# The attention's row stores of a fused attention and mixture-of-experts kernel, issued by ScalarE's queue in place of SyncE's

## The chip, the cores and the metric

The kernel runs on one core of a Trainium2 chip. The metric is the device time of one execution in microseconds (us): before the change it is 562.4 us, the median of 3 runs (560.54 to 562.91).

## The reference

An attention over 32 memory slots per head is computed first, then a top-1 mixture of experts on its output. Shapes: batch 8, 8 heads, 576 tokens, head size 64, so 4608 tokens of 512 numbers; 8 experts with a hidden size of 1024.

```python
a = softmax(phi, axis=2)                       # [8, 8, 576, 32]
k_m = einsum('bhsm,bhsd->bhmd', a, k)          # 32 keys and
v_m = einsum('bhsm,bhsd->bhmd', a, v)          # 32 values per head
attn = softmax(q @ k_m.T / 8)
x = (attn @ v_m).transpose(0, 2, 1, 3).reshape(4608, 512)

logits = x @ w_gate
e_idx = argmax(logits)
gate_w = softmax(logits)[e_idx]
eom = sigmoid(x @ w_output_gate)
for e in range(8):                             # each token goes to one expert
    mask = e_idx == e
    out[mask] = gate_w * eom[:, e] * (relu(x[mask] @ w1[e]) @ w2[e])
```

## The kernel before, in words

**Two parts.** The attention makes the rows of x. They go out to a scratch tensor `xs` in HBM, 576 numbers each (512 of x and gate columns), because the experts need the rows in another order: GpSimd gathers them again by indirect DMAs, sorted by expert (`gather`, L524). The experts' matmuls (`several`, L1216 on) take most of the span and run on TensorE nearly without a gap. The first of them are recorded while the attention's last quarter is still to be done, and the rest of the attention is woven into them by `hook`.

**The attention's loop.** The batch goes in four pairs (`bp`). For a pair, `memory(bp)` (L719) makes the memories: ScalarE takes exponentials of phi (`ph`, L711), TensorE transposes them (L735), ScalarE copies them out (`at`, L745, and `a`, L741 and L742), TensorE sums over the tokens (`sums`, L764, with the loaded keys and values `kvt`), ScalarE scales the sums (`kvm`, L781), TensorE turns them (L790), and ScalarE copies the keys out (`kT`, L795). Beside that runs the loop over 20 query tiles in `attention()` (L1113), five for a pair. One turn of it takes several tiles at different steps, in the order of the table `ORDER` (L35): exponentials (X, `ea`, L875), row maxima (S, L865 to L871), normalising (D, L881 to L884), transposing back (B, L889), the values of a tile in two halves (V0 and V1), and the scores of the next tile (C, L855, which waits for the loaded queries `qt`). M and m are steps of the memories, R steps of the routing, which VectorE and GpSimd do for the most part.

**The rows.** `values` (L892) multiplies a half tile on TensorE (L902) into a PSUM tile `bpd`, and ScalarE copies it to half of the tile `xo` in SBUF (L904). After V1, `store` (L1008) sends the whole `xo` to `xs`: one DMA of 128 partitions x 2 x 576 numbers, 576 KB (L1013), for four of a pair's five tiles, and two DMAs of 64 x 576, 144 KB each (L1017), for the fifth. There are 16 of the former and 8 of the latter. `xo` has two buffers, so the copies of a tile wait until the store of the tile two before has landed.

**What sets the order.** Each engine executes its own instructions in the order in which the code records them, and a waiting instruction holds back all behind it. Every load and store, other than GpSimd's indirect ones, is issued by SyncE (SP), and they run through one hardware queue: queries (`load_q`, L672), keys and values (`load_kv`, L677; a pair of 512 KB loads is issued after each `sums`, two pairs ahead of the one that is summed next), phi (L662), gate columns (L982 and L985, 64-byte pieces), and the experts' weights (L565). The stores stand among them where the code records them. Each such DMA takes the next of eight completion semaphores (DMAHW0 to DMAHW7 in the order's rows), and before it is issued it waits until the last DMA on that semaphore has landed; so at most eight are under way.

Of the kernel before, what the change touches and what calls it, by code (L numbers as in the profile page):

```python
# [17 lines left out]
P = 128  # L18
# [49 lines left out]
def attention_moe(tc, phiT, kv, qT, wgo, wall, out):  # L68
    nc = tc.nc
    V, A, G, T = nc.vector, nc.scalar, nc.gpsimd, nc.tensor  # L70

    with contextlib.ExitStack() as ctx:
        cp = ctx.enter_context(tc.tile_pool(name="cp", bufs=1))
        dp = ctx.enter_context(tc.tile_pool(name="dp", bufs=1, space=bass.MemoryType.DRAM))
        xs = dp.tile([NTOK, XROW], F32, name="xs")
# [932 lines left out]
        def store(bp, c2, xo, lg):  # L1008
            t0 = bp * 2 * S
            b, n = c2 // 2, 2 if c2 < 4 else 1  # L1010
            if c2 < 4:
                r = t0 + b * S + (c2 % 2) * 256
                nc.sync.dma_start(xs[r:r + 256].rearrange("(c p) d -> p c d", p=P),  # L1013
                                  xo[:].rearrange("p c r d -> p c (r d)"))
            else:
                for b_ in range(2):
                    nc.sync.dma_start(  # L1017
                        xs[t0 + b_ * S + 512:t0 + b_ * S + 576],
                        xo[64 * b_:64 * b_ + 64, 0].rearrange("p r d -> p (r d)"))
            xl = xo[:].rearrange("p c r (g d) -> p c (r g) d", g=2)[:, 0:n, :, P:XQ]  # L1020
            defer("lg", lambda: V.tensor_reduce(
                lg[:, 2 * c2:2 * c2 + n], xl.rearrange("p c q l -> p c l q"), axis=AX.X, op=ALU.add))
# [73 lines left out]
        def defer(nm, f):  # L1096
            deferred.append([LATE[nm], f])
# [15 lines left out]
        def attention():  # L1113
# [8 lines left out]
            for t in range(NT + LAG["V"]):  # L1122
                for w in ORDER:
# [8 lines left out]
                    elif w == "W":  # L1132

                        while t == START - 1 and stream.split(2):
                            pass
                    elif w == "V0" and 0 <= g < NT:
                        bp, c = g // 5, g % 5
                        while 2 * bp + (c >= 2) not in ves:
                            mem.step()
                        if g == 5 * bp:  # L1140
                            lgs[bp] = rt.tile([P, NCH, 16], F32, name="lg", bufs=2)
                        xo = wk.tile([P, 2, 2, 2 * XQ], F32, name="xo", bufs=2)
                        values(bp, 2 * c, st[g], xo)
                    elif w == "V1" and 0 <= g < NT:
                        if c < 4:
                            values(bp, 2 * c + 1, st[g], xo)
                        store(bp, c, xo, lgs[bp])
                    elif w == "C" and 0 < g < NT:
                        while 2 * (g // 5) + (g % 5 >= 2) not in kTs:
                            mem.step()  # L1150
                        st[g] = scores(g // 5, g % 5)
                        if g + NQ < NT:
                            load_q(g + NQ)
                    elif w == "S" and 0 <= g < NT:
                        shift(st[g])
                    elif w == "X" and 0 <= g < NT:
                        expo(st[g])
                    elif w == "D" and 0 <= g < NT:
                        divide(st[g])
                    elif w == "B" and 0 <= g < NT:  # L1160
                        back(st[g])
# [282 lines left out]
```

## Time and profile before

| what | value |
|---|---|
| runs | 560.54, 562.91, 562.4 us (median 562.4) |
| the profiled execution's own time | 555.65 us |
| its span on the core | 553.9 us |
| mean granted TensorE clock | 0.969 |
| busy in the span: TensorE, VectorE, ScalarE, GpSimd | 92%, 64%, 52%, 42% |
| moved by DMA | 123.54 MB, 223 GB/s on average |
| on the hardware queue, on GpSimd's queue | 102.71 MB, 20.06 MB |

The span is the profiled execution's on the core; its own time has 1.75 us around that. All rows below are of that one execution, which is 6.75 us shorter than the median of the runs. PE is TensorE's matmuls, PEld its weight loads, DVE VectorE, ACT ScalarE, POOL GpSimd, and SPq the sequencer of SyncE, which issues DMAs and does nothing else. L13 is line 13 of the kernel. A name such as `xo<-bpd` says that the instruction writes tile xo and reads tile bpd.

### The profile page before, as it was taken

How to read it: one execution, taken by the hardware profiler on the slowest of the kernel's cores; microseconds unless marked ns; L12 is line 12 of the kernel's file. 1: busy time of each engine (PE TensorE's matmuls, PEld its weight loads, DVE VectorE, ACT ScalarE, POOL GpSimd, SP SyncE). 2: the span in 40 equal slices, each digit the busy share in tenths (PEclk: the TensorE clock that was granted, in tenths of full speed). 3: DMA queues.
4: the chain of work that ended last, by engine and by line, in shares of the span. 5: the costliest groups of instructions: out<-in, count | busy, mean ns of one | idle time of the engine just before them, and what ended most of it. 6: DMA issues, size and time to landing. Idle time of an engine off the chain costs nothing. (4 is left out here: it accounts for less than half of the span.)

```text
span 553.9 us, 10578 instructions
## 1 busy us (share of the span) xinstructions
PE 509.0 (92%) x3859; PEld 437.6 (79%) x3859; DVE 352.0 (64%) x779; ACT 287.9 (52%) x536; POOL 232.6 (42%) x254
## 2 busy tenths in 40 slices
PE   3788877599999999999999999999999999999993
PEld 2455555388689799898998989897999899888982
DVE  4384979957776659996436556944786387549310
ACT  3475765454454446553435546834775377358310
POOL 2242585851434034410466562563447463710101
PEclk9877989979999999999999999999999999999997
DMA  8999999995457756963547574875586577643001
GB/s 310 416 389 392 411 373 400 320 351 175 132 192 240 225 168 222 309 183 115 154 139 259 174 233 126 262 219 182 179 264 177 190 244 241 201 162 98 30 21 43
DMA packets 41998, 123.54 MB, mean 223 GB/s; under 512 B 10256, under 2 KB 10320, under 8 KB 41552
## 3 DMA queue, kind: packets, MB, share of 16 engines
q1 hardware_dynamic: 35136, 102.71, 56.0%
q0 software_dynamic: 6800, 20.06, 10.3%
q8 instruction: 32, 0.52, 0.4%
q14 instruction: 30, 0.25, 0.1%
HBM read 102.40 MB, written 20.35 MB: 222 GB/s over the span
## 5 line engine op out<-in xcount | busy, mean ns | idle before, releaser
L1275 PE MATMUL bps<-whl,hh 128*128 128x512 f32 x640 | 193.6, 394 | 0.9 <-issue 0.9
L1238 PE MATMUL bps<-xh,whl 128*128 128x384 f32 x640 | 166.0, 336 | 0.0
L590 DVE TENSOR_TENSOR whl<-w,whl 128x1024 fp32r<-128x1024 f32 x112 | 136.1, 1220 | 11.6 <-ACT whl L576 11.2
L1275 PEld LDWEIGHTS bps<-whl,hh 128*128 128x128 f32 x640 | 119.9, 188 | 26.5 <-issue 2.2
L576 ACT CAST whl<-w 128x1024 fp32r<-128x1024 f32 x112 | 116.4, 1044 | 19.3 <-PE bps L1275 14.9
L1238 PEld LDWEIGHTS bps<-xh,whl 128*128 128x128 f32 x640 | 115.8, 188 | 1.3 <-issue 0.6
L531 POOL DMA_INDIRECT xg<-xs,idx_ql x84 | 98.2, 1168 | 25.6 <-issue 23.8
L1238 PE MATMUL bps<-xl,whl 128*128 128x384 f32 x320 | 107.0, 334 | 0.0
L1275 PE MATMUL bps<-whl,hl 128*128 128x512 f32 x240 | 93.8, 391 | 0.5 <-issue 0.5
L1243 DVE SCALAR_TENSOR_TENSOR hl<-bps,hh 128x384 fp32r<-128x384 f32 x80 | 43.9, 554 | 69.9 <-ACT hh L1242 48.1
L1242 ACT ACTIVATE hh<-bps 128x384 fp32r<-128x384 f32 x80 | 38.9, 492 | 85.2 <-PE bps L1238 70.8
L1211 POOL DMA_INDIRECT out<-y,idx_ol x23 | 25.0, 1089 | 113.3 <-ACT y L1210 54.2
L1238 PEld LDWEIGHTS bps<-xl,whl 128*128 128x128 f32 x320 | 60.1, 188 | 0.3
L1275 PEld LDWEIGHTS bps<-whl,hl 128*128 128x128 f32 x240 | 45.1, 188 | 9.1 <-issue 0.8
L871 POOL TENSOR_TENSOR ea<-ea,mx 128x512 f32<-128x512 f32 (+1 forms) x20 | 19.3, 967 | 46.8 <-DVE mx L869 42.4
L1233 PE MATMUL bps<-xh,whl 128*128 128x384 f32 x128 | 37.7, 338 | 0.0
L1234 PE MATMUL bps<-xh,whl 128*128 128x256 f32 x128 | 35.7, 279 | 0.0
L904 ACT COPY xo<-bpd 128x576 f32<-128x576 f32 x36 | 22.6, 639 | 20.6 <-PE bpd L902 11.9
L1210 ACT ACTIVATE y<-bps,gx 128x512 f32<-128x512 f32 x19 | 13.1, 687 | 36.8 <-PE bps L1275 30.1
L1211 POOL DMA_INDIRECT out<-y,idx_ob x9 | 10.0, 1112 | 48.8 <-ACT y L1210 38.0
L902 PE MATMUL bpd<-ve_b,aT 64*128 64x144 f32 (+1 forms) x320 | 27.8, 321 | 3.0 <-DVE ea L865 3.0
L987 POOL TENSOR_SCALAR Aw<-iota_row,row 128x128 bf16<-128x128 bf16 x36 | 25.8, 735 | 8.9 <-DVE row L977 8.9
(263 smaller groups left out, 586.8 us busy)
## 6 DMA issues: line engine op xcount, KB each, us to landing
w<-wall SPq DMA_DIRECT2D x112, 512.0 KB
kvt<-kv SPq DMA_DIRECT2D x32, 512.0 KB
xs<-xo SPq DMA_DIRECT2D x16, 576.0 KB
qt<-qT SPq DMA_DIRECT2D x16, 512.0 KB
ph<-phiT SPq DMA_DIRECT2D x3, 1152.0 KB
kv<-kv SPq DMA_DIRECT2D x4, 512.0 KB
xg<-xs,idx_ql POOLq DMA_INDIRECT x84
ph<-phiT SPq DMA_DIRECT2D x4, 288.0 KB
```

What stands on the lines that cost most here:

```text
L531: G.indirect_dma_start(out=z["xg"][:, k, XQ * b:XQ * b + XQ], out_offset=None, in_=xs[0:z["rows"]].rearrange("t (a q) -> (t a) q", a=4), i ...
L576: A.copy(hl[:, 0], w[:])
L590: V.tensor_tensor(hl[:, 1], w[:], hl[:, 0].bitcast(F32), ALU.subtract)
L902: T.matmul(px[to:to + n, r, sl], z["aT"][h, o:o + n], ves[2 * bp + b][h, g], start=True, stop=True)
L987: (G if AWP else V).tensor_scalar(Aw[:, bp * NCH + c], iota_row[:], row[:, c:c + 1], None, ALU.is_equal)
L1211: G.indirect_dma_start(out=out, out_offset=bass.IndirectOffsetOnAxis(ap=z["idx"][1][0:n, z["q0"] + k:z["q0"] + k + 1], axis=0), in_=y[0:n] ...
L1233: T.matmul(pb, w[:, 0, o:o + P], x[0][:, cc], start=(cc == 0), stop=False)
L1234: T.matmul(pb[:, 0:256], w[:, 1, o:o + P], x[0][:, cc, 0:256], start=False, stop=(cc == 3))
L1238: T.matmul(pb, w[:, b, o:o + P], x[a][:, cc, 0:n_], start=(n == 0), stop=(n == 11))
L1242: A.activation(h_[:, j], pb, AF.Relu)
L1243: V.scalar_tensor_tensor(l_[:, j], pb, 0.0, h_[:, j].bitcast(F32), ALU.max, ALU.subtract)
L1275: T.matmul(py[k], a, w[:, b, DM * f:DM * f + DM], start=(u == 4 and f == 0 and n == 0), stop=(u == 7 and f == 1 and n == len(ps) - 1))
```

## The change

The two calls in `store` that issue the DMAs name ScalarE (`A`) in place of SyncE. Tiles, sizes, destinations and the rest of the code stay.

```diff
             if c2 < 4:
                 r = t0 + b * S + (c2 % 2) * 256
-                nc.sync.dma_start(xs[r:r + 256].rearrange("(c p) d -> p c d", p=P),
+                A.dma_start(xs[r:r + 256].rearrange("(c p) d -> p c d", p=P),
                                   xo[:].rearrange("p c r d -> p c (r d)"))
             else:
                 for b_ in range(2):
-                    nc.sync.dma_start(
+                    A.dma_start(
                         xs[t0 + b_ * S + 512:t0 + b_ * S + 576],
                         xo[64 * b_:64 * b_ + 64, 0].rearrange("p r d -> p (r d)"))
```

On ScalarE, at the end of the first pair and the start of the second, the program before has these rows (the number behind x counts like rows that follow each other; `bpa` and `bpd` are PSUM tiles):

```order
L904 COPY xo<-bpd 128x576 x2
L875 ACTIVATE ea_203<-ea_203 128x16x32
L741 COPY a_874<-bpa 64x256
L742 COPY a_874<-bpa 64x256
L745 COPY at<-bpa 128x512 x2
L904 COPY xo<-bpd 128x576
L875 ACTIVATE ea_204<-ea_204 128x16x32
L745 COPY at<-bpa 128x512
```

The changed program has these in the same place:

```order
L904 COPY xo<-bpd 128x576 x2
L1013 DMA xs<-xo 128x2x576
L875 ACTIVATE ea_203<-ea_203 128x16x32
L741 COPY a_874<-bpa 64x256
L742 COPY a_874<-bpa 64x256
L745 COPY at<-bpa 128x512 x2
L904 COPY xo<-bpd 128x576
L1017 DMA xs<-xo 64x576 x2
L875 ACTIVATE ea_204<-ea_204 128x16x32
L745 COPY at<-bpa 128x512
```

Each store now stands right behind the copies that fill its tile, ahead of exponentials and copies for the next tiles. The order of the compute instructions is the same.

On SP, around the same place, the program before has these rows:

```order
L672 DMA qt<-qT 128x1024
L677 DMA kv_745<-kv 128x1024
L1013 DMA xs<-xo 128x2x576
L677 DMA kvt<-kv 128x1024 x2
L672 DMA qt<-qT 128x512
L1013 DMA xs<-xo 128x2x576
L672 DMA qt<-qT 128x1024
L1017 DMA xs<-xo 64x576 x2
L677 DMA kvt<-kv 128x1024 x2
```

The stores leave that list and nothing comes in their place, so the loads behind a store no longer follow its wait. The semaphores are still given in turn over both engines. On ScalarE, a pair later, the changed program has these rows with their waits:

```order
L904 COPY xo<-bpd 128x576 [waits DMAHW7_49,DVE_49,PE_49]
L1017 DMA xs<-xo 64x576 [waits DMAHW0_49,Activation_49]
L1017 DMA xs<-xo 64x576 [waits DMAHW1_49]
L941 ACTIVATE w__1398<-w__1398 128x72 [waits Pool_49]
L875 ACTIVATE ea_203<-ea_203 128x16x32 [waits DVE_49]
```

On SP, the loads that held the semaphores DMAHW0 and DMAHW1 before those two stores are the first two of these:

```order
L677 DMA kv_1192<-kv 128x1024 [waits DMAHW0_49,PE_49]
L677 DMA kvt<-kv 128x1024 [waits DMAHW1_49]
L677 DMA kvt<-kv 128x1024 [waits DMAHW2_49]
L672 DMA qt<-qT 128x512 [waits DMAHW3_49,PE_49]
L672 DMA qt<-qT 128x1024 [waits DMAHW5_49,PE_49]
```

A store on ScalarE thus waits for ScalarE's own copies (`Activation`) and for the landing of a load that SP has issued earlier.

## Rows read from the trace of the kernel before

**Rows 1.** The page: busy time, share of the span and instructions of each engine; and in 40 equal slices of the span (13.85 us each) the busy share of the DMA engines in tenths and the GB/s that they moved.

```profile
PE 509.0 (92%) x3859; PEld 437.6 (79%) x3859; DVE 352.0 (64%) x779; ACT 287.9 (52%) x536; POOL 232.6 (42%) x254
...
DMA  8999999995457756963547574875586577643001
GB/s 310 416 389 392 411 373 400 320 351 175 132 192 240 225 168 222 309 183 115 154 139 259 174 233 126 262 219 182 179 264 177 190 244 241 201 162 98 30 21 43
```

**Rows 2.** Stretches of the span, from:to in us: its length, then the busy time of each engine with its instructions, the granted clock of TensorE, the DMA engines' busy share and the GB/s.

```profile
40.00:60.00 20.00, 16.97 (x276) 10.86 (x278) 12.32 (x29) 12.90 (x30) 7.82 (x10) 0.83 1.02 394
60.00:80.00 20.00, 15.58 (x316) 10.40 (x306) 16.98 (x50) 12.43 (x30) 13.21 (x21) 0.91 1.04 402
80.00:100.00 20.00, 14.89 (x293) 10.53 (x293) 17.59 (x68) 11.50 (x27) 12.52 (x19) 1.00 1.02 379
100.00:115.00 15.00, 10.05 (x183) 6.74 (x184) 10.63 (x25) 8.00 (x16) 10.76 (x12) 0.83 0.96 337
115.00:140.00 25.00, 24.96 (x177) 22.55 (x176) 19.16 (x36) 12.86 (x22) 7.61 (x8) 0.96 0.64 221
190.00:300.00 110.00, 110.00 (x608) 99.01 (x607) 78.03 (x182) 53.18 (x82) 42.94 (x38) 1.00 0.61 191
```

**Rows 3.** Waits of SP's queue between 36 and 125 us: who waited for whom, us in total, times, the longest in us.

```profile
SPq L1013 <- ACT xo L904: 18.4, 10, 4.2
...
SPq L1017 <- ACT xo L904: 5.8, 2, 3.3
...
SPq L1013 <- DMA qt<-qT: 2.0, 3, 0.9
```

**Rows 4.** The same view between 64 and 66 us, where one load of SP waits for the landing of a store.

```profile
SPq L677 <- DMA xs<-xo: 0.6, 1, 0.6
```

**Rows 5.** The issues of the stores, by line: the time of one in SP's sequencer in ns (shortest, median, longest), and when the first and the last started.

```profile
L1013 SPq DMA_DIRECT2D xs<-xo x16: 377/378/614, 36.9 to 174.6; - x16
L1017 SPq DMA_DIRECT2D xs<-xo x8: 451/532/597, 61.0 to 183.9; - x8
```

**Rows 6.** SP's queue in order of time: start us, us, engine line op out<-in and how many like it in a row.

```profile
37.35 3.13 SPq L677 DMA_DIRECT2D kvt<-kv  x4
...
52.33 0.38 SPq L1013 DMA_DIRECT2D xs<-xo  x1
...
56.67 0.38 SPq L1013 DMA_DIRECT2D xs<-xo  x1
...
79.90 1.80 SPq L677 DMA_DIRECT2D kvt<-kv  x2
...
86.29 1.09 SPq L1017 DMA_DIRECT2D xs<-xo  x2
```

**Rows 7.** TensorE's matmuls in order of time: the same columns, and in brackets the idle time before them in us and what ended it.

```profile
43.61 0.65 PE L764 MATMUL pk<-kvt,at 128*32 128x128 f32 x16 [1.10 <-DMA kvt<-kv]
44.87 0.82 PE L764 MATMUL pk<-kvt,at 128*32 128x128 f32 x16 [0.61 <-DMA kvt<-kv]
...
49.33 2.29 PE L902 MATMUL bpd<-ve_b,aT 64*128 64x144 f32 x16
...
53.90 0.58 PE L790 MATMUL bpa<-ident,kvm 128*128 128x128 f32 x2 [0.27 <-ACT kvm L781]
54.41 1.25 PE L902 MATMUL bpd<-ve_b,aT 64*128 64x144 f32 x16
...
58.03 0.66 PE L735 MATMUL bpa<-ident,ph 128*128 128x128 f32 x4 [0.32 <-ACT a L742]
...
62.75 0.64 PE L764 MATMUL pk<-kvt,at 128*32 128x128 f32 x16 [0.44 <-DMA kvt<-kv]
...
84.22 0.66 PE L735 MATMUL bpa<-ident,ph 128*128 128x128 f32 x4 [0.40 <-ACT a L742]
...
117.08 0.44 PE L1238 MATMUL bps<-xh,whl 128*128 128x384 f32 x1
```

**Rows 8.** ScalarE in order of time, the same columns: what stands behind a store's place, and two pairs of copies.

```profile
37.99 0.59 ACT L745 COPY at<-bpa 128x512 f32<-128x512 f32 x1 [1.10 <-PE bpa L735]
...
42.21 0.59 ACT L745 COPY at<-bpa 128x512 f32<-128x512 f32 x1
...
55.47 1.18 ACT L904 COPY xo<-bpd 128x576 f32<-128x576 f32 x2
...
60.31 0.64 ACT L904 COPY xo<-bpd 128x576 f32<-128x576 f32 x1 [1.00 <-DVE aT L889]
...
61.77 0.59 ACT L745 COPY at<-bpa 128x512 f32<-128x512 f32 x1 [0.29 <-PE bpa L735]
64.34 0.78 ACT L711 ACTIVATE ph<-ph,nmx 128x576 f32<-128x576 f32 x1 [1.99 <-DVE nmx L707]
...
79.15 0.63 ACT L875 ACTIVATE ea<-ea 128x512 f32<-128x512 f32 x1 [1.60 <-POOL ea L871]
...
87.82 0.26 ACT L941 ACTIVATE w__1398<-w__1398 128x72 f32<-128x72 f32 x1 [1.56 <-POOL w__1398 L931]
...
99.66 0.54 ACT L795 COPY kT<-bpa 64x128 f32<-64x128 f32 x2 [0.94 <-PE bpa L790]
...
109.61 0.63 ACT L875 ACTIVATE ea<-ea 128x512 f32<-128x512 f32 x1 [2.39 <-POOL ea L871]
...
126.58 0.49 ACT L1242 ACTIVATE hh<-bps 128x384 fp32r<-128x384 f32 x1 [1.59 <-PE bps L1238]
```

## The prediction

> **What bounds the kernel now.** I read the page first, then the span by stages. The page shows TensorE busy for 92% of the span, and DMA engines that are full for the first nine slices, some 124 us, and half busy later [rows 1]. The stages say where time can be had. From 115 us on TensorE is busy nearly all the time (24.96 of 25 us, then 110.00 of 110), with DMA at 0.61 to 0.64 [rows 2]. So the experts' part is bound by TensorE, and a change of the stores can only move its start. Before 115 us TensorE is busy for 14.89 to 16.97 of 20 us, VectorE for up to 17.59, ScalarE for 11.50 to 12.90, and the DMA engines all the time at 379 to 402 GB/s [rows 2]. No engine is full there; it is a loop of short steps that wait for one another, fed through a full DMA queue. Whatever is won or lost before 115 us is carried to the end one for one.
>
> Then I looked at what the stores do in that loop. Between 36 and 125 us SP stands at them for ScalarE's copies 18.4 us in 10 waits and 5.8 us in 2 [rows 3]. That is much, but SP computes nothing, so it counts only where a load behind it comes late. Landing is slow: a store issued at 56.67 us lets a load of SP go, eight issues on, within the stretch from 64 to 66 us, so it took 7.3 to 9.3 us [rows 4, 6], of which 576 KB at 400 GB/s are about 1.5 us. The rest is the backlog of loads ahead of it. TensorE waits for loads three times after the first store: 1.10 and 0.61 us at 43.61 and 44.87 us, and 0.44 us at 62.75 us [rows 7].
>
> **The change part by part.**
>
> *SP loses the stores.* 16 issues of 0.378 us and 8 of about 0.53 us leave it [rows 5], 10.3 us in all, and so do its waits. The loads behind can be issued up to 4.2 us sooner [rows 3], but as the DMA engines are full they don't land as much sooner. The place where it could count is the stall at 43.61 us: those keys are the first two of four loads begun at 37.35 us [rows 6], right behind the first store, and they land behind its 576 KB, about 1.5 us of the queue. If they are issued ahead of it, they gain between nothing (the store takes its share of the engines all the same) and 1.5 us. What is late next is the tile `at`, which TensorE needs with them: ScalarE copies it at 42.21 us for 0.59 us [rows 8], so it is ready at 42.80, and at 43.3 when a store of 0.5 us stands before it. So 0.3 of the 1.10 us can go, and the 0.61 us behind it; I take 0.8 us, near the most, since SP stood at that store for ScalarE's copies and is now free to issue them first. Of the 0.44 us at 62.75 us I take half, 0.2 us. Gain: 1.0 us, between 0 and 2.15 (all three stalls).
>
> *ScalarE gets them.* The issue of such a DMA has been traced on SP alone, at 0.377 to 0.614 us for the large and 0.451 to 0.597 for the small ones [rows 5]. ScalarE must also let its copies finish: two copies back to back take 1.18 us where one takes 0.64, so 0.1 us of overlap is lost [rows 8]. I take 0.1 + 0.38, some 0.5 us for a large store, and 0.1 + 1.09 = 1.2 us for a pair of small ones (1.09 us is the pair at 86.29 us) [rows 6]; from below nothing excludes that ScalarE goes on at once (0), from above 0.7 us (0.61 + 0.1) and the wait of the rival below. Twelve large stores and two pairs come before 115 us: 12 x 0.5 + 2 x 1.2 = 8.4 us of ScalarE. What of it lies on the path is read from the idle time behind each place. Most are covered: 1.10 us behind the first, 0.29 and 1.99 behind the pair at 61.0 us, 1.60 and 1.56 around 79 and 88 us, 0.94 and 2.39 near 100 and 110 us [rows 8]. If that cover went, the 1.2 us of a pair would be paid in full. Bare are three places where TensorE waits for ScalarE within two us of a store: for `kvm` at 53.90 us (0.27), for `a` at 58.03 (0.32) and at 84.22 us (0.40) [rows 7]. There the whole 0.5 us is added: 1.5 us. At five more stores I read no single cover; as ScalarE is idle for 7 to 8.5 of 20 us [rows 2], I count 0.5 us each as covered there.
>
> *The buffers of xo.* At 60.31 us a copy starts after 1.00 us of idle [rows 8]; it is named after VectorE, yet it also needs the store of 52.33 us [rows 6] to have landed, which after 7.3 to 9.3 us falls at 59.6 to 61.6 us. On a queue of its own a store lands sooner, and no copy should wait for one. I give nothing for it, since 0.29 and 1.99 us of idle follow [rows 8].
>
> *The Trainium skill's page DMA: Bandwidth & Descriptors has a rule against this change* (Issuing engines are not separate DMA queues): DMAs of all issuers run on the same 16 engines and interleave, and another issuer saves the sequencer's time alone. The rows agree as far as they go: the engines are full until 115 us whoever issues [rows 2]. By the rule the gain of 1.0 us falls away and 1.5 us of cost stay, 563.9 us in place of 562.9. The page's Queues, rings and completion order has each engine take turns between the queues, which would let a store overtake the backlog; with one hardware queue in use, no run here shows that yet.
>
> *The experts' part.* Four large stores and two pairs fall after 115 us, 4 x 0.5 + 2 x 1.2 = 4.4 us of ScalarE. It has holes of 1.59 us there before a ReLU [rows 8], TensorE works on without a gap [rows 2], and I cost it at nothing. The cover is the PSUM banks that ScalarE still has to empty; without it the 4.4 us would be the price.
>
> **Sum.** +1.5 - 1.0 = +0.5 us. The profiled execution takes 555.65 us, so it would take 556.2; the median of the runs is 6.75 us above it, and there the forecast is 562.4 + 0.5 = **562.9 us**. A measurement of this kernel tells about 0.5% (2.8 us) from no change, so this is no change. Its own range, with 0 to 2.15 us of gain and 0 to 2.6 us of cost (0.7 us at the three bare places, and at the five others half of the 0.2 us above 0.5), is 560.3 to 565.0 us.
>
> **The rivals.**
>
> *Faster: the stall at 43 us also costs clock, and goes.* While TensorE idles there the clock falls: 0.83 is the mean from 40 to 60 us [rows 2], and sixteen matmuls of L902 take 2.29 us at 49.33 us, 1.25 us at 54.41 [rows 7]. If the keys come earlier and ScalarE's issues cost little, the 1.04 us of that group come back, and about as much again of the three groups of matmuls around it. With the stalls (2.15 us) that is some 4.3 us: 562.4 - 4.3 = 558.1 us. For it: nothing else keeps TensorE waiting there but DMA. Against it: `at` is ready only 0.8 us earlier than the keys, and the idle time that remains may lower the clock as before. Chance 0.25.
>
> *Slower: the store holds ScalarE.* In the changed program a store waits on ScalarE for the landing of a DMA issued earlier on the same semaphore; until then every exponential and copy behind it waits, and TensorE, VectorE and GpSimd with them. The tightest place is the second half of the store at 86.29 us: its semaphore was last held by a load begun at 79.90 us [rows 6], and at 7.3 to 9.3 us of latency that lands at 87.2 to 89.2 us, so ScalarE is held for up to 2.4 us. SP has had such waits at its stores too, 2.0 us in 3 [rows 3]. If a large store costs 1.2 us (0.61 the longest issue, 0.1, and 0.5 of waiting), the bare places cost 3.6 us; the covers are overrun by 0.1 us (1.10), 0.3 us (0.94) and, by pairs of 2.4 us, 0.1 (0.29 and 1.99) and 0.8 us (1.56); and the five other stores pay half of the 0.7 us above 0.5 each, 1.8 us: 3.6 + 1.3 + 1.8 = 6.7 us, and 562.4 + 6.7 = 569.1 us. It decides from about 0.9 us for a large store: 2.7 us at the bare places and 1.0 at the five others are 3.7 us, and less 1.0 us of gain 2.7, the 0.5%. For it: ScalarE is busy for 12.90 of 20 us and within the loop [rows 2]. Against it: at ten of its waits SP was released by the copy and not by a semaphore [rows 3], so most semaphores are free in time. Chance 0.25.
>
> *Nothing at all.* The stores move, but the loads land when the full DMA engines let them, and every issue on ScalarE falls into its idle time: 562.4 us. It lies within the forecast and shares its chance of 0.50.
>
> **How the numbers follow.** No change 0.50 (with 562.9 us the likeliest), faster by over 0.5% 0.25, slower by over 0.5% 0.25. The range reaches to the faster rival's value and a little past it and nearly to the slower one's, 557.5 to 568.5 us, which leaves out about one in ten on either side.
>
> **What would show it.** Right: ScalarE has 24 issues of 0.4 to 0.6 us; a second hardware queue carries 16 x 576 + 8 x 144 KB = 10.6 MB; SP's waits for L904 are gone; the stores land in well under 7 us; the stalls at 43.61 and 44.87 us shrink; TensorE's waits for `kvm` and `a` grow by about 0.5 us each; the experts' first matmul, L1238 at 117.08 us now [rows 7], comes within 2 us of that. Wrong for speed: the clock stays up between 45 and 52 us and it comes at 113 us. Wrong for the worse: ScalarE stands before an L1013 or L1017 for a DMA, or its issues take 0.8 us and more, and it comes after 120 us. The change from 115 us to the end would have to be under 1 us; if it isn't, what I said of the experts' part is wrong.

## The result, and the profile after

The changed kernel takes 564.7 us in the median of 20 runs (561.85 to 570.97), the kernel before 560.11 us beside it (557.45 to 563.6, 20 runs). The ratio is **1.0077, with a 95% interval of 1.005 to 1.0105**: about 4.3 us slower. The ratio leaves out the changed kernel's two longest runs, and the profiled execution is one of them (570.36 us, span 568.6 us). A repeat (the first experiment) has a span of 560.8 us, and what I read below as the cause stands in both.

**The move itself came as described.** The issues, by line, with the time of one in ns (shortest, median, longest) and the first and last start, answer to [rows 5]:

```profile
L1013 ACTq DMA_DIRECT2D xs<-xo x16: 361/366/403, 38.0 to 180.2; - x16
L1017 ACTq DMA_DIRECT2D xs<-xo x8: 452/482/610, 60.5 to 189.4; - x8
```

The page's queues (packets, MB, share of 16 engines) show the second hardware queue with the 10.62 MB of the stores:

```profile
q10 hardware_dynamic: 4992, 10.62, 4.9%
```

**The stretches** (columns as in [rows 2]):

```profile
40.00:60.00 20.00, 15.74 (x320) 9.98 (x310) 13.03 (x30) 14.08 (x34) 9.17 (x12) 1.00 0.90 335
60.00:80.00 20.00, 16.00 (x265) 10.70 (x269) 13.83 (x40) 10.09 (x24) 6.93 (x10) 0.74 1.03 406
...
115.00:140.00 25.00, 23.91 (x184) 21.12 (x185) 18.64 (x33) 13.60 (x26) 8.99 (x10) 0.86 0.80 274
```

Read the last three columns against [rows 2]. From 40 to 60 us the clock is granted in full (0.83 before), but the DMA engines now have holes: 0.90 and 335 GB/s, where they had 1.02 and 394. From 60 to 80 us the clock is 0.74 (0.91 before), and ScalarE and VectorE do some 2.3 and 3.2 us less work.

**Where the time goes: SP's loads now stand for the landing of stores.** SP's waits between 36 and 125 us (total, times, longest), for [rows 3]:

```profile
SPq L672 <- PE bpd L855: 16.3, 5, 5.6
SPq L677 <- DMA xs<-xo: 12.3, 4, 7.5
...
SPq L672 <- DMA xs<-xo: 3.5, 1, 3.5
```

The waits for ScalarE's copies are gone (18.4 and 5.8 us before), but loads wait 15.8 us for stores to land, where they waited 1.7 us before. The 16.3 us in the first row (5.7 before) are waits for a free query buffer: where SP is no longer held at a store, it stands at the next load of queries until TensorE's scores have read the buffer. SP's queue in order of time shows what that does, first in the kernel before, whose rows continue those in [rows 6], then in the changed one:

```profile
42.52 1.38 SPq L677 DMA_DIRECT2D kvt<-kv  x2
...
53.79 0.41 SPq L672 DMA_DIRECT2D qt<-qT  x1
...
57.14 0.45 SPq L672 DMA_DIRECT2D qt<-qT  x1
```

```profile
37.91 8.18 SPq L677 DMA_DIRECT2D kvt<-kv  x2
46.19 1.13 SPq L672 DMA_DIRECT2D qt<-qT  x1
47.42 0.37 SPq L662 DMA_DIRECT2D ph<-phiT  x1
47.84 0.90 SPq L677 DMA_DIRECT2D kvt<-kv  x2
48.84 0.65 SPq L672 DMA_DIRECT2D qt<-qT  x1
49.59 0.67 SPq L677 DMA_DIRECT2D kv<-kv  x1
52.25 3.92 SPq L677 DMA_DIRECT2D kvt<-kv  x2
59.77 0.80 SPq L672 DMA_DIRECT2D qt<-qT  x2
```

The first row covers two loads over 8.18 us, since the second had to wait 7.5 us for the store that ScalarE issued at 37.97: it goes out at 45.76 us, and that store's completion semaphore was full at 45.74. Before, all four of these loads were issued by 40.48 us (37.35 + 3.13, [rows 6]). The change lets SP run past a store's place, but only until the semaphores come round: the eighth DMA recorded after a store waits until that store is issued by ScalarE, however late, and has landed. So the kvt loads of 42.52 us are issued at 47.84 us, 5.3 us later, together with the rest of the backlog. The queries of 53.79 us wait in the same way for the store that ScalarE issues at 49.77 us (landed at 59.70 us), those of 57.14 us stand behind them, and both go out from 59.77 us on.

**ScalarE, at the same time** ([rows 8] has the same places before):

```profile
37.97 0.40 ACTq L1013 DMA_DIRECT2D xs<-xo  x1
...
49.77 0.37 ACTq L1013 DMA_DIRECT2D xs<-xo  x1
...
59.80 0.64 ACT L904 COPY xo<-bpd 128x576 f32<-128x576 f32 x1 [2.15 <-DMA xs<-xo]
60.47 3.95 ACTq L1017 DMA_DIRECT2D xs<-xo  x2
64.47 0.63 ACT L875 ACTIVATE ea<-ea 128x512 f32<-128x512 f32 x1 [4.02 <-DMA kv<-kv]
65.00 0.57 ACT L745 COPY at<-bpa 128x512 f32<-128x512 f32 x1
```

The copy at 59.80 us needs the xo buffer that the store of 49.77 us reads, and waits 2.15 us for it; that store took 9.9 us to land (59.70 us). Then the pair of small stores occupies ScalarE for 3.95 us where two issues take about 1.0: the second one's semaphore was last held by the load of `kv` issued at 49.59 us, which landed at 63.95 us. The exponential and the copy `at` stand behind it for 4 us.

**TensorE** pays for both (brackets as in [rows 7]):

```profile
43.91 0.26 PE L758 MATMUL pk<-zero 1*128 1x256 bf16 x1 [0.54 <-ACT kvm L781]
44.11 1.14 PE L764 MATMUL pk<-kvt,at 128*32 128x128 f32 x32
...
54.12 0.67 PE L855 MATMUL bpd<-qt,kT 64*32 64x256 f32 x16 [0.24 <-ACT xo L904]
...
56.37 0.66 PE L735 MATMUL bpa<-ident,ph 128*128 128x128 f32 x4 [0.72 <-ACT a L742]
...
58.39 0.64 PE L764 MATMUL pk<-kvt,at 128*32 128x128 f32 x16 [0.50 <-DMA kvt<-kv]
60.27 0.65 PE L764 MATMUL pk<-kvt,at 128*32 128x128 f32 x16 [1.24 <-DMA kvt<-kv]
62.41 1.11 PE L855 MATMUL bpd<-qt,kT 64*32 64x256 f32 x16 [1.50 <-DMA qt<-qT]
...
65.70 2.26 PE L764 MATMUL pk<-kvt,at 128*32 128x128 f32 x32 [1.13 <-ACT at L745]
67.89 2.29 PE L902 MATMUL bpd<-ve_b,aT 64*128 64x144 f32 x16
...
72.18 0.46 PE L855 MATMUL bpd<-qt,kT 64*32 64x64 f32 x32
...
122.59 0.61 PE L1238 MATMUL bps<-xh,whl 128*128 128x384 f32 x1
```

And three rows of before that answer to them, the scores (L855) of the eighth, ninth and tenth tile:

```profile
56.16 0.67 PE L855 MATMUL bpd<-qt,kT 64*32 64x256 f32 x16 [0.25 <-ACT xo L904]
...
60.49 0.66 PE L855 MATMUL bpd<-qt,kT 64*32 64x256 f32 x16
...
65.87 0.45 PE L855 MATMUL bpd<-qt,kT 64*32 64x64 f32 x32
```

At the eighth tile the changed kernel is 2.0 us ahead (54.12 against 56.16): the two stalls of 43.61 and 44.87 us are gone (0.54 us for `kvm` stand in their place), and the keys' matmuls run at full clock. At the ninth it is 1.9 us behind, at the tenth 6.3 us. The waits are 0.72 (0.32 before), 0.50, 1.24, 1.50 and 1.13 us, and behind the first four of them the clock is at its lower level: L855 takes 1.11 us at 62.41 us where it took 0.66, 32 matmuls of L764 take 2.26 us where two groups of 16 took 0.65 + 0.64 [rows 7], and L902 2.29 us in place of 1.25. These three rows alone are 2.5 us of the 4.4 us lost between the ninth tile and the tenth. From 40 to 80 us together the mean granted clock is 0.87 in both kernels (0.83 and 0.91 before, 1.00 and 0.74 now): what the clock gave in the first stretch it took back in the second. The delay is then carried: the experts' first L1238 starts at 122.59 us instead of 117.08, 5.5 us later.

### The profile page after: what moved, and what is told of

It reads as the page before. It is cut to its first block, busy times and chain, and to the rows that moved or that the text cites. A ratio compares the mean times of both kernels' runs of the same rounds, so it can differ in the third digit from the quotient of the medians.

```text
span 568.6 us, 10564 instructions
## 1 busy us (share of the span) xinstructions
PE 515.3 (91%) x3859; PEld 439.6 (77%) x3859; DVE 353.9 (62%) x779; ACT 288.0 (51%) x536; POOL 226.1 (40%) x254
## 3 DMA queue, kind: packets, MB, share of 16 engines
q10 hardware_dynamic: 4992, 10.62, 4.9%
## 5 line engine op out<-in xcount | busy, mean ns | idle before, releaser
L1238 PE MATMUL bps<-xh,whl 128*128 128x384 f32 x640 | 166.3, 336 | 0.6 <-issue 0.4
L590 DVE TENSOR_TENSOR whl<-w,whl 128x1024 fp32r<-128x1024 f32 x112 | 137.8, 1235 | 10.2 <-ACT whl L576 10.0
L1238 PEld LDWEIGHTS bps<-xh,whl 128*128 128x128 f32 x640 | 116.0, 188 | 2.2 <-issue 1.5
L1238 PE MATMUL bps<-xl,whl 128*128 128x384 f32 x320 | 107.0, 334 | 0.0
L531 POOL DMA_INDIRECT xg<-xs,idx_ql x84 | 93.1, 1109 | 25.6 <-issue 24.1
L1238 PEld LDWEIGHTS bps<-xl,whl 128*128 128x128 f32 x320 | 60.2, 188 | 0.3
L1275 PEld LDWEIGHTS bps<-whl,hl 128*128 128x128 f32 x240 | 45.5, 190 | 10.7 <-issue 2.2
L871 POOL TENSOR_TENSOR ea<-ea,mx 128x512 f32<-128x512 f32 (+1 forms) x20 | 19.2, 962 | 47.2 <-DVE mx L869 42.9
L902 PE MATMUL bpd<-ve_b,aT 64*128 64x144 f32 (+1 forms) x320 | 29.5, 334 | 3.4 <-DVE ea L865 3.2
L902 PEld LDWEIGHTS bpd<-ve_b,aT 64*128 64x128 f32 (+1 forms) x320 | 22.3, 201 | 9.6 <-DVE ea L865 3.5
```

The lines of the kernel that those rows point to most:

```text
L531: G.indirect_dma_start(out=z["xg"][:, k, XQ * b:XQ * b + XQ], out_offset=None, in_=xs[0:z["rows"]].rearrange("t (a q) -> (t a) q", a=4), i ...
L590: V.tensor_tensor(hl[:, 1], w[:], hl[:, 0].bitcast(F32), ALU.subtract)
L902: T.matmul(px[to:to + n, r, sl], z["aT"][h, o:o + n], ves[2 * bp + b][h, g], start=True, stop=True)
L1238: T.matmul(pb, w[:, b, o:o + P], x[a][:, cc, 0:n_], start=(n == 0), stop=(n == 11))
L1275: T.matmul(py[k], a, w[:, b, DM * f:DM * f + DM], start=(u == 4 and f == 0 and n == 0), stop=(u == 7 and f == 1 and n == len(ps) - 1))
```

## The experiments

Each group of runs has its own runs of the kernel before: 557.21 us for the first four kernels, 554.67 for the next four, 554.58 for the last four. **A** is the theory that stores on ScalarE and loads on SP hold one another by the semaphores they share; **B**, that the issues' own time on ScalarE costs. Later A is split: A1 (semaphores) against A2 (a store lands late, and the two xo buffers with it).

### The changed kernel again

> The changed kernel once more, for a second profile. Theory A (the stores share the eight DMA semaphores with SP's loads, so that ScalarE and SP each stand for landings that the other queue's backlog makes late): again about 1.008 of the kernel before; ScalarE stands for 3 to 5 us at the pair of small stores near 60 us, SP for over 10 us in all for the landing of stores, and the experts' first matmul comes 4 to 7 us later than at 117.08 us. Theory B (the issue's own time on ScalarE, 0.37 us and the end of its copies, is what costs): the same ratio, but no single hold of over 1 us on ScalarE is needed for it. Both: what the first profile lost after 125 us (some 9 us) is not there again, since the profiled execution was one of the longest.

560.98 us against 557.21, ratio **1.0055 (1.0029 to 1.008)**. The stretch from 57 to 72 us repeats: a copy starts at 58.92 us after 2.13 us of waiting for a store, the pair of small stores then takes 3.94 us, SP stands 11.3 us at L677 and 3.8 us at L672 for stores, and the tenth tile's scores start at 71.20 us. The first L1238 is at 121.48 us, 4.4 us later than before.

### One kind of store alone

Only the large stores, or only the small ones, are issued by ScalarE; the other call keeps `nc.sync`:

```diff
e2_large_act, L1013
-                nc.sync.dma_start(xs[r:r + 256].rearrange("(c p) d -> p c d", p=P),
+                A.dma_start(xs[r:r + 256].rearrange("(c p) d -> p c d", p=P),
e3_small_act, L1017
-                    nc.sync.dma_start(
+                    A.dma_start(
```

> Only the 16 large stores (L1013) go to ScalarE; the 8 small ones (L1017) stay on SP. Theory A, with the hold at the pair as the main loss: ScalarE is no longer held for 4 us near 60 us, and most of the loss goes: 0.998 to 1.003 of the kernel before. Theory A, with SP's waits for the landing of the large stores as the main loss: 1.005 to 1.009 stays. Theory B: 12 of the 14 issues before the experts stay, so 1.005 to 1.008.

> Only the 8 small stores (L1017) go to ScalarE; the 16 large ones stay on SP. Theory A, hold at the pair: ScalarE is held at the pair, for as long as the DMA eight issues earlier needs; 1.003 to 1.008. Theory A, large stores: 0.998 to 1.002. Theory B: two pairs before the experts, some 1 us each and mostly covered: 1.000 to 1.002.

Large alone: 562.84 us, ratio **1.0088 (1.0058 to 1.0119)**. Small alone: 562.43 us, **1.0093 (1.0063 to 1.0122)**. Each half costs about as much as the whole, so it is not a sum over issues. With the large ones SP stands 8.8 us at L677 and 7.1 us at L672 for stores. With the small ones ScalarE isn't held at the pair. SP stands 10.7 us in 3 waits at L677 for stores, and one copy waits 3.57 us for the small stores that ScalarE itself issued: the semaphores it waits for are those of the pair, whose second store, issued at 62.03 us, landed at 69.20 us, 7.2 us later. ScalarE's and TensorE's rows of that run:

```profile
61.50 1.14 ACTq L1017 DMA_DIRECT2D xs<-xo  x2
...
69.30 0.64 ACT L904 COPY xo<-bpd 128x576 f32<-128x576 f32 x1 [3.57 <-DMA xs<-xo]
```

```profile
69.99 0.46 PE L855 MATMUL bpd<-qt,kT 64*32 64x64 f32 x32 [3.55 <-ACT xo L904]
```

The tenth tile comes at 70.46 and 69.99 us. The place of the wait moves from one of these three kernels to another; that the tenth tile is late by 4 us or more doesn't.

### Only ScalarE's time

The kernel before, with copies in place of the issues:

```diff
+            if bp < 3:
+                fill = mo.tile([P, DM], F32, name="y", bufs=2)
+                for w in (270,) if c2 < 4 else (270, 390):
+                    A.copy(fill[:, 0:w], xo[:].rearrange("p c r d -> p (c r d)")[:, 0:w])
```

> The kernel before, its stores on SP, with a copy on ScalarE of about 0.4 us (two, 0.8 us, for a fifth tile) put where the changed kernel issues a store, for the first three of four pairs of the batch; the copies go to a tile that nobody reads. It gives ScalarE the issue's time and no wait. Theory B: 1.004 to 1.008 of the kernel before. Theory A: 0.999 to 1.003.

556.71 us, ratio **0.9995 (0.9964 to 1.0025)**. The copies take as much of ScalarE as the issues do, 0.412 to 0.520 us each, and cost at most 1.4 us by the interval (0.25% of 557.21). The tenth tile's scores are at 66.42 us. **B falls.** The first L1238 is a rougher mark than the tenth tile: in this run it starts at 120.19 us, 3.1 us later than in the profile of before, and yet the kernel is no slower.

### Stores from GpSimd, and a third buffer for xo

GpSimd's DMAs have semaphores of their own, so a store issued by it (`G.dma_start` in both calls) shares none with SP's loads. The third buffer takes the space of the experts' gathered rows (`xg` in the rows) while that is empty, here in the first twelve tiles (XO3 = 12):

```diff
-                        xo = wk.tile([P, 2, 2, 2 * XQ], F32, name="xo", bufs=2)
+                        if g % 3 == 2 and g < XO3:
+                            xo = xgs.pools[0][0].tile(xgs.shape, F32, name=xgs.name)
+                            xo = xo[:, 0:2].rearrange("p c (r d) -> p c r d", r=2)
+                        else:
+                            xo = wk.tile([P, 2, 2, 2 * XQ], F32, name="xo", bufs=2)
```

> All 24 stores are issued by GpSimd. They then run on GpSimd's own queue and on its own semaphores, so no load of SP waits for a store's landing by a semaphore and no store for a load's. Theory A1 (the shared semaphores cost the time): SP's waits for xs<-xo at L677 and L672 (11.3 and 3.8 us in the changed kernel) are gone, ScalarE has no wait of 4 us near 60 us, and the time goes back to 0.997 to 1.002 of before, as far as GpSimd's own time for the issues stays beside other work. Theory A2 (a store on a second queue lands late, 8 to 10 us after its issue, and the copies into xo's two buffers wait for it): ScalarE's waits for xs<-xo at L904 stay at 2 to 7 us, the scores of the tenth tile start at 70 us or later (65.9 before), and the ratio stays at 1.004 to 1.010.

> The changed kernel, with a third buffer for xo in the first twelve tiles: every third tile is put in the space of the experts' gathered rows, which stands empty until later. A1 (semaphores): ScalarE still stands some 4 us at the second pair of small stores near 60 us, SP's loads still wait some 10 us for stores, and the ratio stays at 1.004 to 1.010. A2 (buffers): ScalarE's waits for xs<-xo at L904 before 75 us are under 0.5 us together, the scores of the tenth tile start by 68 us, and the ratio falls to 0.996 to 1.003.

> The kernel before, with the same third buffer for xo in the first twelve tiles; stores stay on SP. A1: 0.998 to 1.002, as no copy is held by a buffer there. A2: the 1.00 us before the copy at 60.31 us can go, 0.996 to 1.000. Either way ScalarE has no wait for xs<-xo before 75 us. It is the control of the run of the changed kernel with the third buffer.

> Both at once: stores issued by GpSimd, and a third buffer for xo in the first twelve tiles. Neither shared semaphores nor buffers are left, so A1 and A2 both give 0.994 to 1.002, and the gain of the changed kernel (the clock at 1.00 from 40 to 60 us) should be kept: first L1238 by 116 us where before has 117.08. If it stays at 1.004 or more, a third thing costs the time: a second queue takes DMA time from the loads, or GpSimd's issues cost.

| run | us | ratio, interval | tenth tile's scores |
|---|---|---|---|
| GpSimd | 560.66 | 1.0113 (1.0089 to 1.0138) | 66.61 us |
| ScalarE, three buffers | 559.71 | 1.0087 (1.0058 to 1.0115) | 70.48 us |
| SP, three buffers | 560.71 | 1.011 (1.0082 to 1.0137) | 66.82 us |
| GpSimd, three buffers | 566.14 | 1.0204 (1.0176 to 1.0232) | 66.33 us |

The totals missed, mine for the control above all, and so did A1's 4 us at the pair with three buffers. The third buffer had a price that I hadn't foreseen: in the twelfth tile its space was still being stored when the first gather wanted it. In the run with SP that store was issued at 103.53 us and landed at 112.31 us, which is 8.2 of these 9.2 us; the row names what came last:

```profile
POOL xg L538 <- DMA xs<-xo: 9.2, 1, 9.2
```

But the stretch in question tells A1 from A2. With GpSimd's semaphores SP has no wait for a store left, and the tenth tile is at 66.61 us although ScalarE still waits for xo (3.5 us in 2 waits). With stores on ScalarE and three buffers, ScalarE has no such wait before 75 us, and the pair takes 1.50 us where it took 3.95, yet SP stands 6.8 us at one load of queries for a store, and TensorE waits for keys:

```profile
63.96 0.64 PE L765 MATMUL pk<-kvt,at 128*32 128x128 f32 x16 [1.55 <-DMA kvt<-kv]
65.84 0.64 PE L765 MATMUL pk<-kvt,at 128*32 128x128 f32 x16 [1.24 <-DMA kvt<-kv]
...
70.48 0.46 PE L856 MATMUL bpd<-qt,kT 64*32 64x64 f32 x32
```

(With a line more at the top, L765 and L856 are L764 and L855.) Nor does a second queue as such cost anything there, as far as GpSimd's shows; a second hardware queue without shared semaphores wasn't tried. Where GpSimd's run loses its 1.1% instead isn't settled: its first L1238 starts at 120.31 us and 438.1 us follow, against 117.08 and 436.8 before. What the issues take of GpSimd stands in its own rows: 16 x 0.774 and 8 x 0.573 us, some 17 us, of issues.

```profile
L1013 POOL DMA_DIRECT2D xs<-xo x16: 748/774/950, 37.0 to 184.2; - x16
```

```profile
L1017 POOL DMA_DIRECT2D xs<-xo x8: 531/573/600, 61.9 to 187.1; - x8
```

They stand in line with the subtractions and products of the softmax (L871, L884). That this is what costs the time wasn't tried.

### The third buffer without its price

XO3 = 9, so that the gather finds its space free; stores on ScalarE, and the control with stores on SP:

> As e6_act_xo3, but the third buffer is used in the first nine tiles only, so that the experts' first gather no longer waits for a store from that space. A1 (semaphores): SP still stands 6 us or more for a store's landing between 50 and 70 us, TensorE still waits over 1 us twice for kvt near 64 to 66 us, scores of the tenth tile at 70 us or later, ratio 1.003 to 1.008. A2 (buffers): ratio 0.996 to 1.001, tenth tile by 68 us.

> Its control: the kernel before with the third buffer in the first nine tiles, stores on SP. The 1.1% that e7_sp_xo3 lost came by the first gather's wait of 9.2 us, so both theories say 0.997 to 1.002 here, with the scores of the tenth tile at 65.5 to 67 us.

ScalarE: 558.55 us against 554.58, ratio **1.0069 (1.0042 to 1.0096)**. SP: 553.99 us, **0.9987 (0.9962 to 1.0011)**. As A1 said, and not A2: the buffers cost the kernel before nothing, and give the changed one at most a little back. No copy waits for a buffer before 125 us in this run. ScalarE isn't held at the pair near 61 us, but it is held elsewhere: the store of 80.57 us stands 3.1 us for the landing of a load (80.49 us). SP's waits and TensorE's rows in the run with ScalarE:

```profile
SPq L678 <- DMA xs<-xo: 10.7, 3, 7.5
SPq L673 <- DMA xs<-xg: 7.3, 1, 7.3
```

```profile
65.52 0.64 PE L765 MATMUL pk<-kvt,at 128*32 128x128 f32 x16 [1.33 <-DMA kvt<-kv]
...
68.65 0.45 PE L856 MATMUL bpd<-qt,kT 64*32 64x64 f32 x32
```

68.65 us lies between what A1 (70 or later) and A2 (by 68) had said; the control has 66.15. Of the two waits over 1 us that A1 expected only one came. The clock stayed up here (1.00 from 60 to 80 us), so the size of the loss at this place varies, 2.5 us against 6.3 in the changed kernel.

### Fewer DMAs on the semaphores

Two chunks of keys and values by one DMA of 1 MB, with stores on ScalarE and on SP:

```diff
-            t = ld.tile([P, H, 2 * D], F32, name="kvt" if c < 8 else "kv8", bufs=NKV if c < 8 else 1)
+            if c < 8:
+                if c % 2 == 0:
+                    t = ld.tile([P, 2, H, 2 * D], F32, name="kvt", bufs=NKV // 2)
+                    nc.sync.dma_start(t[:].rearrange("p c h d -> p c (h d)"),
+                                      kv[bp, c:c + 2].rearrange("c p x -> p c x"))
+                    kvts[bp, c], kvts[bp, c + 1] = t[:, 0], t[:, 1]
+                return
+            t = ld.tile([P, H, 2 * D], F32, name="kv8", bufs=1)
             nc.sync.dma_start(t[:], kv[bp, c].rearrange("p (h d) -> p h d", h=H))
```

> The changed kernel with the keys and values loaded two chunks by one DMA of 1 MB in place of two of 512 KB: the same bytes and buffers, but 16 DMAs less on the eight semaphores, so that the DMA whose landing is waited for was issued earlier. A1: ScalarE's wait of 4 us at the second pair of small stores shrinks to under 1.5 us, SP's waits for xs<-xo fall to half or less of 15 us, the scores of the tenth tile start by 69 us, and the ratio to the same kernel with stores on SP (next run) is 0.996 to 1.003. A2: stores land as late as before, ScalarE's waits for xs<-xo at L904 stay at 2 us and more, and the ratio to the next run stays at 1.004 to 1.010. Against before a pair may land up to 1.3 us later for its first half, which can cost both kernels up to 0.5%.

> Its control: the kernel before with the same 1 MB loads, stores on SP. Both theories: SP's own few waits for DMAs at the stores (2.0 us for qt) go, and nothing else changes: 0.996 to 1.005.

ScalarE: 558.4 us, ratio **1.0062 (1.0038 to 1.0085)**. SP: 556.15 us, **1.0028 (1.001 to 1.0047)**. The quotient of the two ratios is 1.0034 (that of the two medians 1.0040), between what A1 (up to 1.003) and A2 (from 1.004) had said. So with 16 DMAs less on the semaphores the move costs about half of what it cost with the third buffer (1.0069 against 0.9987), and less than without either (1.0077 and 1.0055). The pair of small stores holds ScalarE for 1.14 us, and SP's waits for stores fall from 15.8 us to a single one of 6.3, as A1 said; ScalarE's wait for xo stays at 1.9 us (2.4 in the control). But that single one is at the load of phi, and the next keys stand behind it (L771, L862 and L909 are L764, L855 and L902):

```profile
SPq L662 <- DMA xs<-xo: 6.3, 1, 6.3
```

```profile
64.95 1.94 PE L771 MATMUL pk<-kvt,at 128*32 128x128 f32 x32 [4.09 <-DMA kvt<-kv]
66.82 2.29 PE L909 MATMUL bpd<-ve_b,aT 64*128 64x144 f32 x16
...
71.32 0.46 PE L862 MATMUL bpd<-qt,kT 64*32 64x64 f32 x32
```

The control has these rows there:

```profile
63.93 1.08 PE L771 MATMUL pk<-kvt,at 128*32 128x128 f32 x32 [1.47 <-DMA kvt<-kv]
64.94 1.25 PE L909 MATMUL bpd<-ve_b,aT 64*128 64x144 f32 x16
```

So the tenth tile missed the 69 us that I expected; in the control it starts at 67.49 us, 3.8 us earlier. The keys themselves come only 1.0 us later than in the control (64.95 against 63.93). Behind the longer stall the two rows take 1.9 us more, as TensorE runs at the lower clock. The wait has moved; it hasn't gone. None of the variants is faster than the kernel before by more than its interval.

## Why the prediction was wrong in its forecast, and where it was right

The forecast was no change (+0.5 us), and the kernel is slower by 0.77%, some 4.3 us. The median lies in the range given, near the upper end of the forecast's own 560.3 to 565.0 us. But the kernel before ran at 560.11 us in that comparison and not at 562.4, so the change itself was missed by 3.8 us; that the median still lies within the forecast's own range is luck. What came is the rival "the store holds ScalarE", with a chance of 0.25, in a wider form than I gave it. Two of the signs named for the worse came: ScalarE stands before an L1017 for a load, and L1238 starts after 120 us (122.59, and 121.48 in the repeat).

- **The step that failed: "On a queue of its own a store lands sooner, and no copy should wait for one."** Nothing was given for it. By their completion semaphores the first eleven large stores took 3.7 to 9.9 us to land on ScalarE's queue, median 7.1, and 5.4 to 9.5 us on SP's before, median 7.9; I had read 7.3 to 9.3 us off one of these [rows 4, 6]. Another queue brought the landing about 1 us forward (the median in the repeat is 6.7), and the store of 49.77 us, with 9.9 us, held a copy for 2.15 us. By *the Trainium skill's* page DMA: Bandwidth & Descriptors (Queues, rings and completion order) the engines take turns between queues, which I took to say that a store would overtake the backlog. The trace agrees that they take turns, but the store overtakes little: its first packet starts at 53.73 us, 4.0 us after the issue, and from 55 to 60 us its queue starts 63 to 70 packets in a microsecond beside 66 to 80 of SP's. Why the first packet comes so late is open.
- **"The loads behind can be issued up to 4.2 us sooner"** was right for three loads of keys behind the first store (1.6 to 2.9 us sooner) and wrong for the fourth, which is issued 5.7 us later (45.76 against 40.05 us). I had looked at the semaphores for ScalarE's sake alone. They hold SP as well: before, store and load stood in one queue and a load never came to a semaphore whose store hadn't been issued. Now it does, and waits for ScalarE's copies and the landing. How the loss divides between SP's waits and ScalarE's isn't shown. With no buffer waits 1.0069 remains, against 0.9987 for its control, but ScalarE is held there too, 3.1 us before the store of 80.57 us. With the loads of 1 MB ScalarE has no such hold and waits for xo no longer than in the control, and about half of the loss remains beside SP's one wait of 6.3 us.
- **The hold on ScalarE** was priced at 2.4 us for a pair and placed at 86.29 us; it came as 3.95 us at 60.47, since the load that it waits for took 14.4 us (49.59 to 63.95), longer than any landing I had read. The pair of the later place took 1.10 us, unheld.
- **The gain** came, with its clock: no stall at 43.61 and 44.87 us, clock 1.00 to 60 us, 2.0 us ahead at 54.12. What I costed at 0.8 to 1.0 us was 2.0. What the faster rival lacked was the loss of 8.3 us behind it (from 2.0 ahead to 6.3 behind), of which a part is the same clock, lower from 60 to 80 us.
- **The issue's time on ScalarE** was sized well (0.37 us for 0.38, 0.48 for 0.53) and shouldn't have been a cost of 1.5 us: the copies that stand in for it cost nothing measurable. At the three bare places the waits grew by 0.5 us together: for `a` by 0.40 us (0.72 at 56.37) and by 0.11 us (0.51 at 90.38), for `kvm` by 0.03 us (0.30 at 51.88). A fourth place near a store I had overlooked: the 2.28 us for `kvm` at 80.09 us became 3.30 us (85.05), and whether the issue has a part in that isn't shown.
- **The experts' part** at nothing: in the repeat, from the first L1238 to the end is 439.3 us (560.8 - 121.48), before 436.8. In the profiled execution it is 446.0, 9.2 us more. Of the three pairs of kernels that differ in the stores' issuer and are otherwise alike (XO3 = 12, XO3 = 9, loads of 1 MB), none differs by more than 0.5 us there: 434.0, 434.7 and 434.3 us with ScalarE, 434.2, 434.3 and 433.8 us with SP. So nothing speaks for a cost of the stores in that part, and where the profiled execution lost its 9.2 us stays open.
- **The rule that speaks against the change** (*the Trainium skill's* same page, Issuing engines are not separate DMA queues) gave +1.5 us, nearer than mine, but by luck: its 1.5 us are the issues' own price, which the copies in their place don't show. The traces agree with its first half, that other issuers' DMAs interleave on the same engines. Its second, that only sequencer time is saved, leaves out what decided here: the issuers also wait for one another's semaphores.

## What to carry to other kernels

Before a DMA is moved to another engine's queue, count on both queues what its semaphore is shared with: a later DMA of the old queue may then wait for the new engine to issue, and for the landing as well. Read the landing time from the trace of before, and ask what stands behind the wait on each issuer, loads above all. Here the waits of the issuing queue, 24 us at the stores, were not lost time while the DMA engines were full: removing them brought TensorE 2.0 us ahead for a while, and in the run with GpSimd, where no new wait of SP takes their place, the tenth tile comes no earlier than before (66.61 us against 65.87). And a wait of TensorE is to be counted with the clock behind it: in the run with loads of 1 MB keys that came 1.0 us later made the tenth tile 3.8 us later, and 1.9 us of that are two rows at the lower clock.

## What the runs showed of the hardware

- Beside loads that fill the engines, the first eleven stores of 576 KB took 5.4 to 9.5 us to land on SP's queue (median 7.9), 3.7 to 9.9 us on ScalarE's (median 7.1) and 5.1 to 9.7 us on GpSimd's (median 8.2).
- The issue of that store takes 0.37 us on ScalarE, 0.38 on SP and 0.77 on GpSimd.
- A load of 512 KB took 14.4 us from issue to landing as the last of six DMAs that SP issued from 46.19 to 50.26 us; the longest landing in the kernel before is 13.3 us.
